# Attention ordered by whole batches, in 24 steps of one 288-column score tile, ahead of the expert layers

## The chip, the cores and the metric

The kernel runs on one core of a Trainium2 chip. The core has five engines that run side by side, each through its own list of instructions in order: TensorE (PE, matrix products; PEld is its weight load), VectorE (DVE), ScalarE (ACT), GpSimd (POOL) and SyncE (SP), which here issues nearly all DMAs. The metric is device time in microseconds (us), the median of three runs. A profiled execution adds a trace, whose span runs from the first to the last of the program's own instructions. TensorE's clock has two levels, 1.2 and 2.4 GHz; the profile gives it as PEclk, a share of the upper one.

## The reference

Two batches of 8 heads, 576 positions, 64 numbers per head, all float32. Heads 0 to 3 are local (a query sees itself and the 31 keys before it), heads 4 to 7 strided (a query sees earlier keys whose position is the same modulo 32). The attention output, 1152 tokens of 512 numbers, goes through a mixture of four experts and then through a gated layer.

```python
mask_local   = (rel >= 0) & (rel < 32)
mask_strided = (rel >= 0) & (pos[None, :] % 32 == pos[:, None] % 32)
attn = softmax(where(mask, scale * q @ k.T, -1e9))
x = attn @ v                              # -> (1152, 512)
for e in range(4):                        # w1[e]: 512x1024, w2[e]: 1024x512
    out += p[:, e:e + 1] * (relu(x @ w1[e]) @ w2[e])
return (sigmoid(out @ w_gate) * (out @ w_val)) @ w_out   # float64 weights, width 1536
```

## The kernel before, in words

**Products.** Each factor of the expert and gate products is scaled by a power of two and split into a high and a low float16 part, and each product is three matmuls (high by high, high by low, low by high; `split_products`, lines 585 to 587). There are 4560 of these, called products below; all but 336 have 288 columns.

**Units.** The tokens form four chunks T of 288. The products come in 56 units, each written as a generator: ("u", s, T) is the first matrix of expert s (or, from s = 4 on, the gate and value matrices), ("d", s, T) the second. A u unit has 8 tiles of 12 products, a d unit of an expert 4 tiles of 24, so 96 products each. Units are numbered in program order: 0 to 7 are expert 0 (u and d of chunk 0, then of chunk 1, and so on); from 8 on the u unit of one chunk is followed by the d unit of an earlier one. A tile ends in its evacuation from PSUM: in a u unit ACT writes the high part and a float32 copy and POOL the low part (lines 624 to 626); in a d unit DVE scales the tile (line 645) and, from expert 1 on, POOL adds it to the sum `x2acc` (line 647).

**Weights.** Weight pieces (0 and 1 are the matrices of expert 0, 2 and 3 of expert 1, up to 7; 8 to 16 are the float64 thirds of the gated layer) are prepared by `prep_weights`, a generator of which `prep_some` advances up to two steps per call, at one point of every tile. A piece of an expert takes four maxima on DVE (line 308, two per 1 MB half `raw`), then a step that folds them (line 310), a PE transpose of the result (line 246), a PE product that spreads it (line 252), and then the conversion of four parts of 1024 columns: ACT scales, ACT casts to the high part, POOL subtracts for the low part (lines 339, 340, 342). The four steps around the transpose return "hold", which ends that call. Only three halves fit in the `raw` buffers, so the second half of a piece is loaded into the place of a half of the piece before, when that has been converted. The prepared weights live in two pools of two places; `has_room` holds a piece back until the unit number has passed `free_after`, the last use of the piece whose place it takes. For the second pool's first two pieces (2 and 3) that is N_ATT - 1, here 5.

**Attention.** It runs as a generator of steps, one `attend()` each. Step i normalizes the tile of step i-1, multiplies by the values for a step four (or three) back, transposes the weights of the step three (or two) back, transposes q and k of a later step, and computes the scores of its own. One step's softmax is a chain: a mask and the scores on PE into one PSUM tile, row maximum and subtraction on DVE (lines 413, 414), exponential on ACT, row sum, an added constant and a reciprocal on DVE (lines 457 to 459), multiplication by it on POOL (line 460). Attention is cut by chunk: chunk 0 takes 4 tiles-steps and a drain and stands alone at the start; the other chunks' steps are laid into units 0 to 3, one after every 6 (later 9) groups of three products. Local heads take 96 queries by 128 keys, one score tile per head, so two tiles to a step. In the stretch ahead of unit 0 each step is followed by 6 matmuls on zeros (`keep_warm`, line 170). `x_pair` scales a chunk's attention output and splits it (lines 517, 518).

**Loads.** q, k and v come by chunk; for local heads with 256-byte pieces. SP takes its DMAs strictly in order. The token weights `pb` (line 221) sit in four buffers, and a later one waits on SP until DVE has read the one whose place it takes.

Of the kernel before, what the change touches and what calls it, by code (L numbers as in the profile page):

```python
# [26 lines left out]
PSUM_BUFS = 3  # L27
PB_BUFS = 4
ATT_LATER = 9
WARM = 11  # L30
WARM_STEP = 6
ATT_EVERY = 6
# [3 lines left out]
def attn_moe_glu_kernel(ctx, tc, q, k, v, dp, w1, w2, wg, wv, wo, out):  # L36
# [13 lines left out]
    TL = TC // 3  # L50
# [6 lines left out]
    accp = ctx.enter_context(tc.tile_pool(name="accp", bufs=1))  # L57
# [8 lines left out]
    sp_ = at_stack.enter_context(tc.tile_pool(name="sps", bufs=2, space=PSUM, side="right", reuse_waits="tile"))  # L66
# [5 lines left out]
    def load_strided_qk(T, c):  # L72

        b, part = divmod(T, 2)
        h0 = 4 + 2 * c
        for nm, src in (("qs", q), ("ks", k)):
            t = atp.tile([NC, 2, 8 * D], F32, tag=nm, name=nm, bufs=3)
            nc.sync.dma_start(
                t, src[b, h0:h0 + 2, part * TC:(part + 1) * TC].rearrange("h (u r) d -> u h (r d)", r=8))
            qkv[nm, T, c] = t  # L80

    def load_strided_v(T, eng):
        b, part = divmod(T, 2)
        for c in range(2):
            h0 = 4 + 2 * c
            if part == 0:
                qkv["vs", b, c] = atp.tile([NU, 2, 8 * D], F32, tag="vs", name="vs", bufs=3)
            eng.dma_start(
                qkv["vs", b, c][part * NC:(part + 1) * NC],
                v[b, h0:h0 + 2, part * TC:(part + 1) * TC].rearrange("h (u r) d -> u h (r d)", r=8))  # L90

    def load_local(T, c, eng):

        b, part = divmod(T, 2)
        for nm, src in (("ql", q), ("kl", k)):
            t = qkv[nm, T, c] = atp.tile([TL, 3, 2, D], F32, tag=nm, name=nm, bufs=2)
            for x in range(2):
                eng.dma_start(
                    t[:, :, x, :], src[b, 2 * c + x, part * TC:(part + 1) * TC].rearrange("(i p) d -> p i d", p=TL))

    def load_vl(T, eng):

        b, part = divmod(T, 2)
        t = atp.tile([128, 4, 3, D], F32, tag="vl", name="vl", bufs=2)
        for h in range(4):
            i0 = 0
            if part == 0:
                eng.dma_start(t[:, h, 0, :], v[b, h, 0:128, :])
                i0 = 1
# [344 lines left out]
    def group_norm(g):  # L454
        for pp, sm, n, w, m, to_sum in soft[g]:
            if to_sum:
                nc.vector.tensor_reduce(sm, pp, AX.X, ALU.add)
# [496 lines left out]
```

## Time and profile before

| what | value |
|---|---|
| time, median of 3 runs | 778.07 us (775.97 to 778.96) |
| profiled execution, its own time | 779.5 us |
| span of the profiled execution | 777.7 us |
| PE, DVE, ACT, POOL busy | 719.1, 387.5, 296.2, 306.6 us |
| mean granted TensorE clock | 0.95 of 2.4 GHz |
| bytes moved by DMA | 48.76 MB, 63 GB/s over the span |

Matmuls overlap in the pipeline, so a PE that reads as busy can still run at half its clock; the granted clock has to be read beside it. The busy share is a mean over stages that differ, so the stages are what to read: the stretch ahead of the first product, the units that share PE with attention, and the rest.

### The profile page before, as it was taken

The numbers are of one execution on the slowest core, as the hardware profiler recorded it, in microseconds if no ns is written. First come the engines' busy times: TensorE is split into PE (matmuls) and PEld (weight loads), VectorE is DVE, ScalarE is ACT, GpSimd is POOL, SyncE is SP. The second block draws the span as 40 slices with busy tenths as digits, with TensorE's granted clock in tenths as the row PEclk, the third lists the DMA queues.
The fourth block names the chain that finished last, engine by engine and source line by source line (L and its number), as shares of the span: only waits on it lengthen the run. The fifth ranks groups of instructions, "written<-read, shape, count | busy, mean of one in ns | idle before, by whom it ended". The sixth has DMA issues, their size and how long they took to land.

```text
span 777.7 us, 13784 instructions
## 1 busy us (share of the span) xinstructions
PE 719.1 (92%) x5727; PEld 528.1 (68%) x5727; DVE 387.5 (50%) x778; ACT 296.2 (38%) x618; POOL 306.6 (39%) x326
## 2 busy tenths in 40 slices
PE   8886788999988899979999998987989999999998
PEld 5545566677766677757777776765766666676774
DVE  2755365453224141125821967575967967922122
ACT  1343643353374841634315232522333344141220
POOL 2213631231374873735835554534142433231110
PEclk7988696999999999989999999899999999999999
DMA  8705451000033330030410213030303211000001
GB/s 175 182 10 162 114 133 35 1 2 8 9 109 116 109 117 8 1 116 15 167 52 9 84 41 109 2 108 1 109 1 109 64 46 55 1 1 1 28 28 69
DMA packets 34590, 48.76 MB, mean 63 GB/s; under 512 B 18684, under 2 KB 21024, under 8 KB 34528
## 3 DMA queue, kind: packets, MB, share of 16 engines
q1 hardware_dynamic: 33312, 47.59, 20.2%
q8 instruction: 45, 0.74, 0.4%
q10 hardware_dynamic: 1216, 0.30, 0.2%
q14 instruction: 17, 0.14, 0.1%
HBM read 45.50 MB, written 2.38 MB: 62 GB/s over the span
## 4 chain that ended last, share of the span: by engine, by line
PE 65%; DVE 14%; POOL 7%; ACT 6%; DMA 4%; issue 3%; SPq 0%; POOLq 0%; DVEq 0%; ACTq 0%
PE gps L585 19%; PE gps L586 19%; PE gps L587 18%; POOL wl L342 4%; DMA raw<-in_moe_w_dram 3%; DVE pk L308 3%; POOL hl L626 2%; POOL x2acc L647 2%; PE sps L402 1%; PE o L501 1%; DVE cv L279 1%; PE warm L170 1%; DVE bits L275 1%; ACT wh L340 1%; DVE bits L277 1%
## 5 line engine op out<-in xcount | busy, mean ns | idle before, releaser
L585 PE MATMUL gps<-xh,wh 128*128 128x288 f16 x896 | 263.1, 294 | 2.1 <-ACT xh L517 2.1
L586 PE MATMUL gps<-xl,wh 128*128 128x288 f16 x896 | 263.0, 294 | 0.3 <-DVE xl L518 0.3
L587 PE MATMUL gps<-xh,wl 128*128 128x288 f16 x896 | 262.7, 293 | 0.0
L586 PEld LDWEIGHTS <-wh 128*128 128x128 f16 x1408 | 140.4, 100 | 40.1 <-issue 2.4
L587 PEld LDWEIGHTS <-wl 128*128 128x128 f16 x1408 | 140.4, 100 | 39.2 <-issue 1.1
L585 PEld LDWEIGHTS <-wh 128*128 128x128 f16 x1408 | 140.1, 99 | 39.4 <-issue 0.3
L626 POOL TENSOR_TENSOR hl<-t,hh 128x288 f16<-128x288 f32 x128 | 100.7, 795 | 130.8 <-ACT t L625 121.7
L586 PE MATMUL gps<-hl,wh 128*128 128x288 f16 x512 | 148.0, 289 | 0.3 <-POOL hl L626 0.2
L585 PE MATMUL gps<-hh,wh 128*128 128x288 f16 x512 | 148.1, 289 | 0.0
L587 PE MATMUL gps<-hh,wl 128*128 128x288 f16 x512 | 148.0, 289 | 0.0
L624 ACT ACTIVATE hh<-gps 128x288 f16<-128x288 f32 x128 | 52.3, 409 | 165.3 <-PE gps L587 165.2
L723 POOL TENSOR_TENSOR hl<-t,hh 128x288 f16<-128x288 f32 x48 | 37.5, 781 | 139.7 <-ACT hh L722 139.7
L342 POOL TENSOR_TENSOR wl<-raw,wh 128x1024 f16<-128x1024 f32 x30 | 65.2, 2175 | 17.5 <-ACT wh L340 14.7
L645 DVE SCALAR_TENSOR_TENSOR t<-gps,comb,pb 128x288 f32<-128x288 f32 x48 | 24.6, 513 | 93.5 <-PE gps L587 86.9
L647 POOL TENSOR_TENSOR x2acc<-x2acc,t 128x288 f32<-128x288 f32 x48 | 40.3, 840 | 63.7 <-DVE t L645 60.1
L625 ACT ACTIVATE t<-gps 128x288 f32<-128x288 f32 x128 | 51.9, 405 | 14.5 <-POOL hl L626 14.5
L308 DVE TENSOR_REDUCE pk<-raw 128x1 f32<-128x1024 f32 x32 | 37.6, 1210 | 34.2 <-DMA raw<-in_moe_w_dram 34.2
L460 POOL TENSOR_TENSOR P<-P,sm 96x384 f32<-96x384 f32 (+1 forms) x28 | 21.0, 755 | 84.8 <-DVE sm L459 62.6
L722 ACT CAST hh<-t 128x288 f16<-128x288 f32 x48 | 20.7, 431 | 80.8 <-DVE t L721 80.8
L721 DVE SCALAR_TENSOR_TENSOR t<-gps,sg 128x288 f32<-128x288 f32 x48 | 21.8, 455 | 54.7 <-PE gps L587 42.1
L342 POOL TENSOR_TENSOR wl<-cv,wh 128x1024 f16<-128x1024 f32 x18 | 40.1, 2226 | 19.1 <-ACT wh L340 19.1
L714 ACT ACTIVATE sg<-gps,comb 128x288 f32<-128x288 f32 x48 | 23.9, 499 | 47.8 <-PE gps L587 39.1
(125 smaller groups left out, 869.1 us busy)
## 6 DMA issues: line engine op xcount, KB each, us to landing
raw<-in_moe_w_dram SPq DMA_DIRECT2D x16, 1024.0 KB
raw<-in_moe_w_gate_dram SPq DMA_DIRECT2D x6, 1024.0 KB
raw<-in_moe_w_val_dram SPq DMA_DIRECT2D x6, 1024.0 KB
raw<-in_moe_w_out_dram SPq DMA_DIRECT2D x6, 1024.0 KB
pb<-pd SPq DMA_DIRECT2D x15, 144.0 KB
out_dram<-outacc SPq DMA_DIRECT2D x8, 256.0 KB
qs<-in_q_dram SPq DMA_DIRECT2D x8, 144.0 KB
ks<-in_k_dram SPq DMA_DIRECT2D x8, 144.0 KB
```

Of the source, the lines that this page charges most:

```text
L308: nc.vector.tensor_reduce(pk[:, n:n + 1], part, AX.XY, ALU.max, apply_absolute_value=True)
L342: nc.gpsimd.tensor_tensor(lo_, part, hi_, ALU.subtract)
L585: nc.tensor.matmul(ps, ah, bh, start=i == 0, stop=False)
L586: nc.tensor.matmul(ps, ah, bl, start=False, stop=False)
L587: nc.tensor.matmul(ps, al, bh, start=False, stop=i == n - 1)
L624: nc.scalar.activation(hh[fb], ps, AF.Relu, scale=DOWN)
L625: nc.scalar.activation(t, ps, AF.Relu, scale=DOWN)
L626: nc.gpsimd.tensor_tensor(hl[fb], t, hh[fb], ALU.subtract)
L645: nc.vector.scalar_tensor_tensor(t, ps, cc, pb[e, T], ALU.mult, ALU.mult)
L647: nc.gpsimd.tensor_tensor(a, a, t, ALU.add)
L714: nc.scalar.activation(sg, pg, AF.Sigmoid, scale=comb[:, col:col + 1])
L723: nc.gpsimd.tensor_tensor(dl, gv, dh, ALU.subtract)
```

## The change

Attention is cut by batch instead of by chunk. Each batch has 12 steps (strided heads in three steps per pair, local heads in three steps per pair), each with one score tile of 288 columns: 24 steps, with no drain between batches. A local tile now holds 64 queries by 96 keys of both heads of a pair. Local q and k are loaded in pieces of 1536 bytes, six positions to a partition; their transposition is six plain products with the identity per half, and the copies out of PSUM put the positions in order. All of batch 0 (steps 0 to 17, with the first steps of batch 1) stands ahead of unit 0, with 5 matmuls on zeros after each step; ten more steps go into unit 0, one after every 3 groups of three products; what is left runs before unit 1. `x_pair` now serves two chunks with one scale.

Besides: the low part of an expert's weights is made on DVE in one instruction from the raw half, so ACT does one instruction per part and POOL none; the sum `x2acc` is added on DVE; N_ATT is 1, so pieces 2 and 3 have room from unit 1 on; PSUM has 2 instead of 3 banks for products and 3 instead of 2 for scores while attention lasts.

```diff
-PSUM_BUFS = 3
+PSUM_BUFS = 2
-ATT_LATER = 9
-WARM_STEP = 6
-ATT_EVERY = 6
+WARM_STEP = 5
+ATT_EVERY = 3
+BLOCK = 64
+LEAD = 32
...
+    def load_local_qk(b, c):
+        for nm, src in (("ql", q), ("kl", k)):
+            t = qkv[nm, b, c] = atp.tile([TL, 2, 6 * D], F32, tag=nm, name=nm, bufs=2)
+            nc.sync.dma_start(t, src[b, 2 * c:2 * c + 2].rearrange("h (p i) d -> p h (i d)", i=6))
...
             hi_, lo_ = wh[i][at], wl[i][at]
-            if early and n % 2 == 0:
+            if dt == F32:
                 nc.scalar.activation(hi_, part, AF.Copy, scale=up[:, i:i + 1])
                 nc.vector.scalar_tensor_tensor(lo_, part, up[:, i:i + 1], hi_, ALU.mult, ALU.subtract)
                 yield
...
+                    pv_ = ps[:, :3 * TL].rearrange("p (i n) -> p i n", i=3)
+                    for x in range(3):
+                        i = 3 * half + x
+                        for y in range(2):
+                            nc.tensor.matmul(
+                                pv_[64 * y:64 * y + 64, x, :], src[:, y, i * D:(i + 1) * D], ident[:TL, :TL],
+                                start=True, stop=True)
+                    frm = ps[:, :3 * TL].rearrange("p (i n) -> p n i", i=3)
+                    dst = to[:, :S].rearrange("p (n i) -> p n i", i=6)[:, :, 3 * half:3 * half + 3]
+                if nm == "q":
+                    nc.scalar.activation(dst, frm, AF.Copy, scale=SCALE)
+                else:
+                    nc.vector.tensor_copy(dst, frm)
+                yield
...
+        for b in range(B):
+            for c in range(2):
+                tasks.append((len(gs), qk_tasks("s", b, c)))
+                gs += [("s", b, c, 0, (0, 1)), ("s", b, c, 1, (0,)), ("s", b, c, 1, (1,))]
+            for c in range(2):
+                tasks.append((len(gs), qk_tasks("l", b, c)))
+                gs += [("l", b, c, t, (0, 1)) for t in range(3)]
+        n = len(gs)
+        ends = {n // B * (b + 1) - 1 + 4: b for b in range(B)}
...
+            if 0 <= i - 1 < n:
+                norm(gs[i - 1])
+            if 0 <= i - 4 < n:
+                values(gs[i - 4])
+            if 0 <= i - 3 < n:
+                transposes(gs[i - 3])
+            do_tasks(i)
+            if i < n:
+                scores(gs[i])
...
             if e:
-                nc.gpsimd.tensor_tensor(a, a, t, ALU.add)
+                nc.vector.tensor_tensor(a, a, t, ALU.add)
...
-    N_ATT = len(units) - 2
+    N_ATT = 1
...
         while 0 not in x_done:
             i = attend()
             keep_warm(WARM_STEP)
-            for _ in range(2):
-                if i >= 3 and (going or todo[0] == 0):
-                    prep_some(0, 1)
-        keep_warm(WARM_STEP)
+            if i >= 8 and (going or todo[0] == 0):
+                prep_some(0, 1)
         for n, u in enumerate(units):
-            while u[2] not in x_done:
-                attend()
+            if n == 1:
+                while "p" not in tmp:
+                    if attend() is None:
+                        end_attention()
...
-                    if n_none % (ATT_LATER if 1 in x_done else ATT_EVERY) == 0 and attend() is None:
+                    if n_none % ATT_EVERY == 0 and attend() is None:
                         end_attention()
```

How the change moves instructions is seen at three places. The first is PE's list inside unit 0, at the first step that is laid between products. Before, it is a step of chunk 1 (a strided tile, and transposes of local q and k):

```order
L472 MATMUL tps<-ident,P 72x128 x4
L384 MATMUL qkps<-ident,ql 128x96 x3
L384 MATMUL qkps<-ident,kl 128x96 x3
L398 LDWEIGHTS identb
```

Now it is step 18, of batch 1:

```order
L459 MATMUL o<-PT,vs 64x36 x16
L433 MATMUL tps<-ident,P 36x128 x8
L371 MATMUL qkps<-ident,ql 64x96 x6
L371 MATMUL qkps<-ident,kl 64x96 x6
L393 LDWEIGHTS identb
L393 MATMUL sps<-ml,identb 128x288
L407 MATMUL sps<-klT,qlT 64x96 x6
```

Such a step stands after every 9 products of unit 0 instead of after every 18 of units 0 to 3, and it holds one score tile whether its heads are local or strided.

The second place is SP's list of DMAs around the last weights of the experts (`raw` from `in_moe_w_dram`; 128x4x512 are halves of a second matrix, 128x2x1024 of a first one). Before:

```order
L138 DMA raw<-in_moe_w_dram 128x4x512
L221 DMA pb<-pd 128x288 x3
L138 DMA raw<-in_moe_w_dram 128x4x512
L138 DMA raw<-in_moe_w_gate_dram 128x2x512
L221 DMA pb<-pd 128x288
```

And now:

```order
L126 DMA raw<-in_moe_w_dram 128x4x512
L212 DMA pb<-pd 128x288 x2
L126 DMA raw<-in_moe_w_dram 128x4x512
L126 DMA raw<-in_moe_w_gate_dram 128x2x512
L212 DMA pb<-pd 128x288 x2
```

The second half of piece 7 (the second `raw` row of each) stood behind three loads of `pb` and now stands behind two; the third, which waits for the end of unit 14, comes after it.

The third place is DVE's list in unit 26, the d unit of the last expert and chunk 0, with its last tile and the maximum over the chunk. Before:

```order
L645 SCALAR_TENSOR_TENSOR t<-gps,comb,pb 128x288
L649 TENSOR_REDUCE peak<-x2acc 128x1
L657 TENSOR_REDUCE peak<-peak 128x1
```

And now:

```order
L611 SCALAR_TENSOR_TENSOR t<-gps,comb,pb 128x288
L613 TENSOR_TENSOR x2acc<-x2acc,t 128x288
L615 TENSOR_REDUCE peak<-x2acc 128x1
L623 TENSOR_REDUCE peak<-peak 128x1
```

The addition, which stood on POOL between the first two rows, is now DVE's own.

## Rows read from the trace of the kernel before

**Rows 1.** Windows by stage: length, busy (count) by PE, PEld, DVE, ACT, POOL; clock.

```profile
0.00:53.70 53.70, 45.97 (x399) 27.75 (x400) 25.69 (x65) 18.06 (x42) 9.06 (x27) 0.87 0.58 133
53.70:184.10 130.40, 111.47 (x1097) 82.73 (x1097) 66.48 (x178) 54.41 (x143) 40.69 (x49) 0.84 0.26 67
184.10:443.40 259.30, 244.59 (x1943) 191.65 (x1941) 96.11 (x152) 116.60 (x230) 145.93 (x141) 0.97 0.20 67
443.40:583.80 140.40, 127.10 (x987) 98.20 (x985) 98.81 (x201) 47.77 (x96) 60.63 (x60) 0.96 0.16 54
583.80:777.70 193.90, 189.94 (x1310) 127.80 (x1307) 100.43 (x186) 59.41 (x109) 50.30 (x51) 1.00 0.11 40
269.80:281.60 11.80, 11.80 (x99) 9.43 (x97) 3.75 (x5) 7.23 (x9) 11.35 (x8) 1.00 0.27 91
```

**Rows 2.** Timeline of PE: start, length, line, operation; steps ahead of unit 0.

```profile
11.67 2.74 PE L170 MATMUL warm<-const-float32-0.0 128*128 128x512 bf16 x6
...
24.52 1.13 PE L501 MATMUL o<-PT,vs 36*64 36x36 f32 x32
25.57 1.05 PE L472 MATMUL tps<-ident,P 128*36 128x128 f32 x8
26.46 0.49 PE L427 MATMUL sps<-ml,identb 96*96 96x384 bf16 x2
26.88 0.90 PE L431 MATMUL sps<-klT,qlT 64*96 64x128 f32 x12
27.71 1.48 PE L170 MATMUL warm<-const-float32-0.0 128*128 128x512 bf16 x6
...
38.72 0.68 PE L368 MATMUL qkps<-ident,qs 36*128 36x36 f32 x8
...
44.58 0.72 PE L402 MATMUL sps<-ksT,qsT 64*64 64x72 f32 x16
```

**Rows 3.** Groups by line and shape on DVE: busy us, mean ns, idle before.

```profile
L308 DVE TENSOR_REDUCE pk<-raw 128x1 f32<-128x1024 f32 x32 | 37.6, 1210 | 34.2 <-DMA raw<-in_moe_w_dram 34.2
...
L518 DVE SCALAR_TENSOR_TENSOR xl<-xf,up,xh 128x288 f16<-128x288 f32 x16 | 7.6, 532 | 6.2 <-ACT xh L517 6.2
L414 DVE TENSOR_TENSOR P<-sps,nm 128x288 f32<-128x288 f32 x12 | 5.5, 458 | 1.5 <-DVE nm L413 0.5
...
L413 DVE TENSOR_REDUCE nm<-sps 128x4 f32<-128x288 f32 x8 | 3.6, 450 | 3.8 <-PE sps L402 3.7
L457 DVE TENSOR_REDUCE sm<-P 128x4 f32<-128x288 f32 x8 | 3.5, 440 | 0.5 <-ACT P L415 0.5
...
L336 DVE SCALAR_TENSOR_TENSOR wl<-raw,up,wh 128x1024 f16<-128x1024 f32 x2 | 2.6, 1285 | 2.8 <-ACT wh L335 2.8
...
L459 DVE RECIPROCAL sm<-sm 128x4 f32<-128x4 f32 x8 | 1.4, 178 | 0.3
```

**Rows 4.** Timeline: a PE transpose in unit 8; SP's loads of token weights.

```profile
245.96 0.37 PE L246 MATMUL gps<-ident,pk 128*1 128x128 f32 x1 [3.54 <-DVE pk L310]
...
282.37 47.88 SPq L221 DMA_DIRECT2D pb<-pd  x3
```

**Rows 5.** Timeline: DVE, POOL, PE after unit 26's last product (479.3).

```profile
480.92 0.51 DVE L645 SCALAR_TENSOR_TENSOR t<-gps,comb,pb 128x288 f32<-128x288 f32 x1
...
481.50 0.79 POOL L647 TENSOR_TENSOR x2acc<-x2acc,t 128x288 f32<-128x288 f32 x1 [2.32 <-DVE t L645]
...
482.33 0.45 DVE L649 TENSOR_REDUCE peak<-x2acc 128x1 f32<-128x288 f32 x1 [0.90 <-POOL x2acc L647]
...
483.12 0.27 PE L246 MATMUL gps<-ident,peak 128*1 128x128 f32 x1 [2.31 <-DVE peak L657]
```

**Rows 6.** Timeline: one DVE line, with POOL at work and without.

```profile
469.66 2.12 POOL L626 TENSOR_TENSOR hl<-t,hh 128x288 f16<-128x288 f32 x2
...
471.22 1.11 DVE L277 SCALAR_TENSOR_TENSOR bits<-raw,bits 128x512 uint32<-128x512 uint32 x1
...
479.59 0.68 DVE L277 SCALAR_TENSOR_TENSOR bits<-raw,bits 128x512 uint32<-128x512 uint32 x1
```

More of the change, by code (lines that the diff above doesn't have):

```diff
@@ L92, in load_local @@
[L92 to L109, printed above, removed]
-            k0 = part * TC + 96 * i0 - 32
-            src = v[b, h, k0:k0 + 128, :]
-            eng.dma_start(t[:, h, i0:3, :], bass.AP(src.tensor, src.offset, [[D, 128], [96 * D, 3 - i0], [1, D]]))
-        qkv["vl", T] = t
+            t = qkv[nm, b, c] = atp.tile([NU, 2, 8 * D], F32, tag=nm, name=nm, bufs=2)
@@ L395, in scores_strided, with scores @@
+    def scores(g):
+        kind, b, c, part, hs = g
+        if kind == "s":
+            w = NC * (part + 1)
+            m = 4 * len(hs)
+            mask = (mask_s2 if part else mask_s)[:, :w].unsqueeze(1).to_broadcast([128, m, w])
+        else:
+            w, m = WIN, 3
+            mask = mask_l[:, 0 if part == 0 else 1:, :][:, :3, :]
         ps = sp_.tile([128, 512], F32, tag="s", name="sps")
         pv_ = ps[:, :m * w].rearrange("p (a b) -> p a b", b=w)
-        mask = (mask_s2 if part else mask_s)[:, :w]
@@ L409, in scores_strided @@
-        nm = atp.tile([128, 8], F32, tag="nm", name="nm", bufs=4)
-        sm = atp.tile([128, 8], F32, tag="sm", name="sm", bufs=6)
-        pt = atp.tile([128, 384], F32, tag="P", name="P", bufs=6)
+        nc.tensor.matmul(pv_, identb, mask, start=True, stop=False)
+        qt, kt = QT[kind, b, c], KT[kind, b, c]
+        for j in range(m):
+            for x in range(2):
+                lo = 64 * x
+                rows = slice(lo, lo + 64)
+                if kind == "s":
+                    at = (4 * hs[0] + j) * NU
+                    lhsT = qt[rows, at + part * NC:at + part * NC + 64]
+                    rhs = kt[rows, at:at + w]
+                else:
+                    at = (3 * part + j) * BLOCK
+                    lhsT = qt[rows, at:at + BLOCK]
+                    rhs = kt[rows, at:at + w]
+                nc.tensor.matmul(pv_[rows, j, :], lhsT, rhs, start=False, stop=j == m - 1)
@@ L553, in attention, with do_tasks @@
+        n = len(gs)
+        ends = {n // B * (b + 1) - 1 + 4: b for b in range(B)}
+        running = []
+        def do_tasks(i):
+            left = 2
+            while tasks and (tasks[0][0] <= i + 1 or (tasks[0][0] <= i + 3 and left > 0)):
+                if next(tasks[0][1], "end") == "end":
+                    tasks.pop(0)
+                else:
+                    left -= 1
+        do_tasks(-1)
+        for i in range(n + 8):
             for x in list(running):
@@ L913, in attn_moe_glu_kernel @@
                 go_late(NT - 1)
-                acc["out"] = accp.tile([128, NTB, DM], F32, tag="acc", name="outacc")
+                acc["out"] = tmp["acc"].tile([128, NTB, DM], F32, tag="acc", name="outacc")
             load_p_some(n)
```

367 lines of the change are left out of this document (145 added, 222 removed).

## The prediction

> **What bounds the kernel now.** I read the stages first [rows 1], because the busy shares of the whole span mix a PE that is full with one that waits. The last row there, one d unit with nothing around it, is the measure: 96 products, PE busy 11.80 of 11.80 us, clock 1.00. A unit costs 11.8 us when nobody waits. The stage from 583.8 on has clock 1.00 and PE busy 189.94 of 193.90 us; the change does not reach it, so it stays 193.9. The 34 units before it would take 34 x 11.8 = 401.2 us, but end at 583.8. The other 182.6 us lie in four places: 53.7 ahead of the first product; 130.4 - 47.2 = 83.2 in units 0 to 3, which share PE with attention; 259.3 - 236.0 = 23.3 in units 4 to 23; 140.4 - 118.0 = 22.4 in units 24 to 33.
>
> In the first two stages the clock is 0.87 and 0.84 and PE is busy 45.97 of 53.70 and 111.47 of 130.40 us. PE works most of the time there, but a good part of it at the lower clock, and stops to wait for the softmax of a step. The nine steps ahead of unit 0 cost 6.0 us each, the 21 in units 0 to 3 on average 83.2 / 21 = 4.0 us.
>
> In units 4 to 23, PE, which takes its list in order, stands at the transpose of a weight piece's maxima until DVE has them [rows 4]: 3.54 us in unit 8. There are four such waits (units 6, 8, 9, 15). With the lower clock that follows some of them they make up most of the 23.3 us, so 5.8 each. In unit 15 the cause is on SP: three loads of `pb`, which must wait for a reader, occupy the queue from 282.37 for 47.88 us, and the weights behind them come late.
>
> In units 24 to 33 PE waits for the maximum of an expert sum [rows 5]: 2.31 us in unit 27, one of four (units 27, 29, 30, 32). The chain hands the tile from DVE to POOL and back, and DVE sits idle 0.90 us at every tile meanwhile, so that it begins the last tile 1.6 us after PE has finished (480.92 against 479.3).
>
> **The start, ahead of unit 0.** Now 18 steps stand there instead of nine. PE's prices at the upper clock [rows 2]: 32 value products 1.05 us (from one row's start to the next), 8 transposes of weights 0.9, a mask 0.2, 12 local scores 0.83, 16 strided scores 0.7 (32 short ones I take as 1.1), 5 matmuls on zeros 1.2 (6 take 1.48), 4 transposes of q or k 0.35. A half of local q or k is now six plain products, which no row shows; between 0.35 and the 0.90 of local scores, I take 0.6, since they have fewer columns than those scores.
>
> Before, the first zeros begin at 11.67. Two more copies of q and k now precede them: 13.7. At the lower clock the zeros of step 0 cost 2.3 (6 took 2.74), step 1 costs 3.2 and 2.3 more for zeros, then step 2 at the upper clock 2.1: 23.6. Steps 3 to 7, added from the list, are 4.6, 4.8, 2.6, 5.4 and 4.9, together 22.3, and DVE has less than that: 45.9.
>
> From step 8 on the first weight piece is prepared beside attention and DVE has more than PE. Each of the ten steps 8 to 17 has a maximum 0.45, subtraction 0.46, sum 0.44 and two short ones of about 0.2, so 1.75 [rows 3], 17.5 in all; four weight maxima at 1.21 are 4.8; three low parts at 1.29, 3.9; four splits of x at 0.53, 2.1; eight copies out of PSUM, priced like the subtraction, 3.7; three maxima over 576 columns at 0.9, 2.7; small ones 2. That is 36.7 us against 33 for PE from the list. Each engine also waits for the other. In the first stage before, time over PE busy was 53.70 / 45.97 = 1.17 [rows 1]; with that factor 43 us. The first product comes at 89, 35 us later than before.
>
> **Unit 0.** Ten steps, 18 to 27, one per 9 products. PE: 11.8 for products and 16 for attention, 28. DVE has 33 before unit 1 may begin: six full steps 10.5, one sum 0.9, four splits 2.1, six weight maxima 7.3, five low parts 6.4, four copies 1.9, three wide maxima 2.7, small ones 1.2. With 1.17: 38 us. Unit 1 begins at 127. The last two splits of x run under its products. Before, four units had been done by 184.1; now units 1 to 3 add 35.4, so the same point comes at 162 without further waits.
>
> **Weights.** An expert's piece loses one ACT instruction and the POOL subtraction per part; DVE gets one of 1.29 us instead. It needs two calls for conversion, not four. POOL's hand-over leaves the chain, and pieces 2 and 3 need not wait for unit 6. What decides is the distance on PE between the call that converts the half whose place is reused and the transpose behind it. By the order of the program it is 96 products or more for pieces 2, 4, 5, 7 and 8 (11.8 us) and 60 (7.4 us) for piece 3, in unit 2, and piece 6, in unit 9. In between must fit the conversion of two parts (2.6 on DVE after ACT), the load and two maxima (2.4). The load's time is the unknown; I expect 7.4 to be too short and 11.8 enough, so two waits of 5.8 remain: one in units 1 to 3, one in units 4 to 23. The bounds are no wait at all and one for each of five pieces, 0 to 29 us. In SP's list piece 7's second half no longer stands behind the `pb` load that waited for unit 14, so unit 15's wait goes.
>
> The DVE instruction reads two tiles in SBUF while POOL works on the low parts of a unit. The trace shows what that can cost [rows 6]: the same DVE instruction takes 0.68 us alone and 1.11 beside POOL, 0.43 more. On four parts that is 1.7 us per piece, which counts only in the two waits: 3 us in all, within the range.
> The Trainium skill, page "SBUF — State Buffer", section "Who interferes with whom", says that DVE with two SBUF inputs and GpSimd share a port, and that whichever starts second is blocked until the first is done. The two rows agree; by that rule the sum below would be about 3 us higher.
>
> **The addition on DVE.** It costs 48 times about 0.46 (like the subtraction of the same size), with no wait behind it in experts 1 and 2. In expert 3, scaling 0.51, addition 0.46 and maximum 0.45 follow each other without the idle 0.90. DVE is then on time at the last tile, and the chain ends 1.7 us after the last product instead of 3.8. In units 27 and 29 twelve products, 1.5 us, cover it, so these waits and their lower clock go; in units 30 and 32 nothing stands between, and about 2 us remain. With waits for gate weights left as they are, I take 12 instead of 22.4 us (bounds 5 and 22.4).
>
> **Sum.** 127 + 35.4 + 5.8 (units 1 to 3), 236 + 5.8 + 0.8 (4 to 23), 118 + 12 (24 to 33), 193.9 behind: 734.7 us of span. The profiled execution's own time was 1.8 above its span and the median of the runs 1.4 below that execution, so 735.
>
> **Rivals.**
> 1. *PE alone sets the pace.* If DVE's work hides, the factor falls away: 23.6 + 22.3 + 33 + 28 = 107 for the start and unit 0, 20 us less, 715. For it: in steps at the upper clock without weights PE runs from group to group without a gap [rows 2]. Against it: DVE's list is the longer one from step 8 on.
> 2. *Steps cost what they cost.* A step is a chain over four engines; with before's 6.0 us per step ahead of unit 0 and 4.0 inside, the first product comes at 108 and unit 1 at 108 + 11.8 + 40 = 160: 768. For it: both averages are measured. Against it: they hold two score tiles per local step, drains and late loads.
> 3. *The waits stay.* The loads remain late and DVE, which took over POOL's work, is late itself: 23.3 and 22.4 as before instead of 6.6 and 12, nothing saved there: 27 us more, 762.
> 4. *Slower: the clock stays low while attention lasts.* PE's short float32 pieces with waits between them ran at 0.84 to 0.87 before [rows 1]. At 1.2 GHz throughout, steps 3 to 17 take 2 x 55 and unit 0 2 x 28: unit 1 begins at 190 and the time is 798. It decides from a begin of unit 1 at 127 + 43 = 170 on. Against it: 5 matmuls on zeros in every step, and no long idle on PE by the sums above.
>
> **How the numbers follow.** Forecast 0.52 (its own range 722 to 750), rival 1 0.12, rival 2 0.16, rival 3 0.13, rival 4 0.06, no change to speak of 0.01. The range 715 to 767 holds the forecast and rival 3, about half of rival 1 and most of rival 2, so eight in ten; the ends leave out the corners where several bounds fall together. Less than 0.5% either way, 4 us, cannot be told from no change. Faster 0.91, same 0.03, slower 0.06.
>
> **What would show it.** First product near 89 and first product of unit 1 near 127: the start and unit 0 are right. A clock above 0.9 in the first 89 us: rival 4 is out. In units 1 to 23, PE waits at the piece transposes in units 2 and 9 alone. At the transposes of the expert maxima in units 27 and 29 waits under 0.5 us, in 30 and 32 about 2. The stage after unit 33 at 193.9. The prediction is wrong if unit 1 begins after 150, or if DVE, with POOL's work on top, makes PE wait where it did not before.

## The result, and the profile after

The changed kernel takes 735.62 us (median of 4 runs, 735.24 to 741.38) where the kernel before took 777.58 in the same comparison (775.97 to 778.96): a ratio of 0.948, 95% interval 0.943 to 0.953. The forecast was 735. The profiled execution took 735.24 us, its span is 733.5. One of the six runs of the experiment called unit 0's front, at 746.44 us, was in a slower state and is left out of its median below.

The stages, from the windows of both traces [rows 1] and the forecast's sum:

| stage | before | forecast | after |
|---|---|---|---|
| ahead of the first product | 53.7 | 89 | 79.9 |
| unit 0 | | 38 | 44.9 |
| units 1 to 3 | | 41.2 | 40.8 |
| all up to unit 4 | 184.1 | 168.2 | 165.6 |
| units 4 to 23 | 259.3 | 242.6 | 241.5 |
| units 24 to 33 | 140.4 | 130 | 131.6 |
| behind unit 33 | 193.9 | 193.9 | 194.8 |

The windows of the changed kernel, the stages first and then three pieces of the first one (the low clock, steps 3 to 7, steps 8 to 17), with the columns of [rows 1] (start:end, length, busy time of PE, PEld, DVE, ACT, POOL, granted clock, DMA share, GB/s):

```profile
0.00:79.90 79.90, 73.40 (x949) 49.66 (x962) 49.44 (x130) 27.20 (x62) 16.47 (x46) 0.98 0.53 139
79.90:124.80 44.90, 34.77 (x431) 25.43 (x431) 37.33 (x78) 22.29 (x53) 10.46 (x16) 0.94 0.31 108
124.80:165.60 40.80, 37.37 (x296) 28.95 (x296) 29.92 (x50) 17.66 (x33) 8.73 (x9) 0.99 0.30 104
165.60:407.10 241.50, 238.10 (x1937) 189.18 (x1936) 104.17 (x176) 82.41 (x194) 73.50 (x89) 1.00 0.17 55
407.10:538.70 131.60, 122.50 (x986) 96.02 (x984) 109.14 (x220) 47.35 (x96) 44.24 (x39) 1.00 0.17 58
538.70:733.50 194.80, 190.00 (x1310) 127.84 (x1308) 101.10 (x187) 59.84 (x110) 50.62 (x51) 1.00 0.11 40
...
9.80:13.20 3.40, 3.07 (x21) 1.99 (x18) 1.74 (x5) 0.76 (x2) 0.53 (x1) 0.50 0.94 241
17.10:39.30 22.20, 21.47 (x335) 15.62 (x338) 13.09 (x34) 6.81 (x16) 3.78 (x9) 1.00 0.94 232
39.30:79.90 40.60, 36.80 (x493) 25.11 (x498) 29.97 (x79) 16.38 (x38) 6.45 (x14) 1.00 0.16 47
```

The clock column and the PE column are to be read together. From unit 1 on the clock is 0.99 to 1.00; before it was 0.84 to 0.97 up to unit 33. POOL's 145.93 us in units 4 to 23 have become 73.50, and PE waits less although DVE has more to do. The first stage is a PE stage: busy 73.40 of 79.90 us. Unit 0 is the only stage in which DVE is busier than PE.

What PE waited for in units 1 to 23 (us in total, times, longest), from the view of waits:

```profile
PE gps L237 <- DVE pk L301: 5.1, 3, 2.8
PE gps L552 <- POOL hl L592: 1.7, 1, 1.7
```

The transposes at line 237 are those of the weight pieces; their three waits lie in units 2 (1.7), 9 (2.8) and 15 (0.6). Unit 8, which waited 3.54 us [rows 4], has none.

Three places from the timelines of ACT, DVE and PE:

```profile
83.70 2.17 ACT L325 ACTIVATE wh<-raw,up 128x1024 f16<-128x1024 f32 x2
85.78 1.80 ACT L489 ACTIVATE xh<-xf,up 128x288 f16<-128x288 f32 x4
87.49 0.67 ACT L438 COPY PT<-tps 36x288 f32<-36x288 f32 x2
87.91 0.91 PE L371 MATMUL qkps<-ident,ql 96*64 96x96 f32 x12 [3.40 <-ACT PT L438]
...
119.28 2.34 DVE L299 TENSOR_REDUCE pk<-raw 128x1 f32<-128x1024 f32 x2
121.53 0.74 DVE L475 TENSOR_REDUCE peak<-xf 128x1 f32<-128x576 f32 x1
122.31 0.16 DVE L480 TENSOR_REDUCE peak<-peak 128x1 f32<-128x4 f32 x1
122.52 0.37 PE L237 MATMUL peaks<-ident,peak 128*1 128x128 f32 x1 [3.44 <-DVE peak L480]
...
442.75 0.69 DVE L270 SCALAR_TENSOR_TENSOR cv<-magn,bits 128x512 f32<-128x512 uint32 x1
443.36 0.51 DVE L611 SCALAR_TENSOR_TENSOR t<-gps,comb,pb 128x288 f32<-128x288 f32 x1
443.90 0.46 DVE L613 TENSOR_TENSOR x2acc<-x2acc,t 128x288 f32<-128x288 f32 x1
444.40 0.45 DVE L615 TENSOR_REDUCE peak<-x2acc 128x1 f32<-128x288 f32 x1
444.88 0.16 DVE L623 TENSOR_REDUCE peak<-peak 128x1 f32<-128x4 f32 x1
445.19 0.27 PE L237 MATMUL gps<-ident,peak 128*1 128x128 f32 x1 [0.69 <-DVE peak L623]
```

At 83.70 two conversions of weights and four splits of x stand in ACT's list ahead of the copies that empty PSUM, and PE waits 3.40 us. At 119.28 two maxima of the next weight piece stand ahead of the maximum that PE waits for, 3.44 us. Both are in unit 0. The last six rows answer to [rows 5]: scaling, addition and maximum follow on one engine, without the idle 0.90 us of the hand-over, and the wait in unit 27 is 0.69 instead of 2.31.

### The profile page after: what moved, and what is told of

It is laid out like the page before. It is cut to its first block, busy times and chain, and to the rows that moved or that the text cites. A ratio compares the mean times of both kernels' runs of the same rounds, so it can differ in the third digit from the quotient of the medians.

```text
span 733.5 us, 13980 instructions
## 1 busy us (share of the span) xinstructions
PE 696.1 (95%) x5899; PEld 517.1 (70%) x5911; DVE 431.1 (59%) x836; ACT 256.7 (35%) x544; POOL 204.0 (28%) x249
## 3 DMA queue, kind: packets, MB, share of 16 engines
HBM read 45.63 MB, written 2.38 MB: 65 GB/s over the span
## 4 chain that ended last, share of the span: by engine, by line
PE 77%; DVE 15%; ACT 5%; issue 2%; POOL 1%; ACTq 0%; DVEq 0%; POOLq 0%
PE gps L551 22%; PE gps L552 22%; PE gps L553 21%; DVE pk L299 3%; PE warm L158 3%; PE sps L407 2%; DVE wl L326 2%; ACT wh L325 2%; PE qkps L371 1%; PE tps L433 1%; DVE cv L270 1%; PE o L459 1%; DVE x2acc L613 1%; DVE t L611 1%; DVE bits L268 1%
## 5 line engine op out<-in xcount | busy, mean ns | idle before, releaser
L552 PE MATMUL gps<-xl,wh 128*128 128x288 f16 x896 | 256.7, 286 | 1.1 <-DVE xl L490 1.1
L551 PE MATMUL gps<-xh,wh 128*128 128x288 f16 x896 | 256.9, 287 | 0.3 <-ACT xh L489 0.3
L553 PE MATMUL gps<-xh,wl 128*128 128x288 f16 x896 | 256.6, 286 | 0.0
L592 POOL TENSOR_TENSOR hl<-t,hh 128x288 f16<-128x288 f32 x128 | 105.0, 825 | 247.8 <-ACT t L591 247.6
L553 PEld LDWEIGHTS <-wl 128*128 128x128 f16 x1408 | 138.0, 98 | 38.2 <-issue 3.2
L551 PEld LDWEIGHTS <-wh 128*128 128x128 f16 x1408 | 137.8, 98 | 36.1 <-issue 0.2
L552 PEld LDWEIGHTS <-wh 128*128 128x128 f16 x1408 | 137.9, 98 | 35.6 <-issue 0.8
L689 POOL TENSOR_TENSOR hl<-t,hh 128x288 f16<-128x288 f32 x48 | 37.5, 782 | 145.4 <-ACT hh L688 145.4
L611 DVE SCALAR_TENSOR_TENSOR t<-gps,comb,pb 128x288 f32<-128x288 f32 x48 | 24.6, 513 | 83.6 <-PE gps L553 82.1
L326 DVE SCALAR_TENSOR_TENSOR wl<-raw,up,wh 128x1024 f16<-128x1024 f32 x32 | 40.8, 1314 | 35.7 <-ACT wh L325 35.7
L551 PE MATMUL gps<-wh,hh 128*128 128x512 f16 (+1 forms) x112 | 41.6, 371 | 0.0
L552 PE MATMUL gps<-wl,hh 128*128 128x512 f16 (+1 forms) x112 | 41.6, 371 | 0.0
L553 PE MATMUL gps<-wh,hl 128*128 128x512 f16 (+1 forms) x112 | 41.6, 371 | 0.0
```

Source lines behind the costliest of these rows:

```text
L326: nc.vector.scalar_tensor_tensor(lo_, part, up[:, i:i + 1], hi_, ALU.mult, ALU.subtract)
L551: nc.tensor.matmul(ps, ah, bh, start=i == 0, stop=False)
L552: nc.tensor.matmul(ps, ah, bl, start=False, stop=False)
L553: nc.tensor.matmul(ps, al, bh, start=False, stop=i == n - 1)
L592: nc.gpsimd.tensor_tensor(hl[fb], t, hh[fb], ALU.subtract)
L611: nc.vector.scalar_tensor_tensor(t, ps, cc, pb[e, T], ALU.mult, ALU.mult)
```

## The experiments

Each time stands beside runs of the kernel before; the ratio to it has its 95% interval. The stages of each run come from its own trace. The changed kernel's own ratio is 0.948 (0.943 to 0.953).

**One part undone: the addition on POOL.**

```diff
-                nc.vector.tensor_tensor(a, a, t, ALU.add)
+                nc.gpsimd.tensor_tensor(a, a, t, ALU.add)
```

> The changed kernel, except that the sum x2acc is added on POOL again. Theory (the hand-over from DVE to POOL and back made PE wait at the maxima of the expert sums): the waits at the transposes of these maxima grow again by 1.5 to 2 us each in units 27, 29, 30 and 32, with some time at the lower clock behind them; units 24 to 33 go from 131.6 back to 138 to 141 us, the rest stays (units 4 to 23 at 241.5), time 742 to 745. Rival (units 24 to 33 got shorter because POOL no longer has the low parts of the weights, and DVE or POOL is on time anyway): units 24 to 33 stay at 131 to 133, time 735 to 737.

Measured 746.61 us, ratio 0.960 (0.955 to 0.966). Window of units 24 to 33:

```profile
408.30:547.80 139.50, 127.23 (x987) 98.19 (x985) 98.79 (x201) 47.78 (x96) 60.36 (x60) 0.96 0.16 55
```

139.5 instead of 131.6, units 4 to 23 at 240.7. The waits at the maxima are 10.3 us in all instead of 6.2, and the granted clock is 0.96 instead of 1.00. The theory holds for these units (138 to 141 expected), though the median lies above its 742 to 745. Of the 7.9 us, 3.2 are more idle time of PE and 4.7 more busy time, with three stretches at the lower clock. The wait of 0.61 us in unit 15 is absent in this run: it is what the addition costs when it stands on DVE.

**One part undone: low parts of weights by ACT, ACT, POOL.**

```diff
-            if dt == F32:
+            if early and n % 2 == 0:
                 nc.scalar.activation(hi_, part, AF.Copy, scale=up[:, i:i + 1])
```

> The changed kernel, except that the low part of an expert's weights is made as before by two ACT instructions and a subtraction on POOL, so that a part takes two advances of the generator again. Theory (the number of advances decides how far apart conversion, load and transpose stand on PE): pieces 2 and 3 move from units 2 and 3 to units 3 and 4, pieces 5 and 6 each get one more tile of distance, and the transpose in unit 9 stands 96 products behind the one in unit 8 as after the change; single waits of 1 to 3 us appear or grow, units 4 to 23 go from 241.5 to 244 to 252 us. Unit 0 gets longer by 2 to 6 us, because ACT, which already makes PE wait there, has one more instruction of about 1 us per part. Units 24 to 33 stay at 131.6. Time 739 to 750. Rival (what helped in units 4 to 23 was the earlier room for pieces 2 and 3 and nothing else): units 4 to 23 stay at 241 to 243, unit 0 alone grows, time 736 to 741. Other rival (DVE is the crowded engine and gains from giving the work away): unit 0 gets shorter by 2 to 5 us, time 730 to 734.

Measured 766.37 us, ratio 0.984 (0.978 to 0.990): more than any theory gave. Units 4 to 23 take 259.5, all that the change had gained there, units 1 to 3 46.1 and unit 0 47.1. Timelines of POOL, SP, DVE and PE, in units 8, 9 and 14:

```profile
221.11 4.27 POOL L332 TENSOR_TENSOR wl<-raw,wh 128x1024 f16<-128x1024 f32 x2 [1.38 <-ACT wh L330]
230.52 0.34 SPq L212 DMA_DIRECT2D pb<-pd  x1
231.40 0.93 SPq L126 DMA_DIRECT2D raw<-in_moe_w_dram  x2
237.30 2.35 DVE L299 TENSOR_REDUCE pk<-raw 128x1 f32<-128x1024 f32 x2 [4.56 <-DMA raw<-in_moe_w_dram]
239.89 0.37 PE L237 MATMUL gps<-ident,pk 128*1 128x128 f32 x1 [4.08 <-DVE pk L301]
...
249.17 2.14 POOL L332 TENSOR_TENSOR wl<-raw,wh 128x1024 f16<-128x1024 f32 x1
251.34 5.93 SPq L126 DMA_DIRECT2D raw<-in_moe_w_dram  x2
256.32 2.34 DVE L299 TENSOR_REDUCE pk<-raw 128x1 f32<-128x1024 f32 x2 [10.03 <-DMA raw<-in_moe_w_dram]
...
315.66 9.05 POOL L332 TENSOR_TENSOR wl<-raw,wh 128x1024 f16<-128x1024 f32 x4 [1.38 <-ACT wh L330]
316.31 1.80 DVE L613 TENSOR_TENSOR x2acc<-x2acc,t 128x288 f32<-128x288 f32 x1
```

This is the path of a piece. Two subtractions on POOL free a half, a load takes its place, DVE reads it, and PE waits for DVE. Two different steps hold it up. In unit 8 the half is free at 225.38, but its load leaves only at 231.40, because a `pb` load stands ahead of it on SP, and that one waits until DVE has read the last tile of unit 7 (to 230.49). Units 4 and 15 are alike. These three units are 4.4, 6.9 and 5.4 us longer than in the changed kernel, 16.7 of the 18.0 us that units 4 to 23 lose. In unit 9 no `pb` load is in the way: the load leaves 0.03 us after the second subtraction, so there the conversion itself is on the path, and unit 9 is 1.3 us longer. For two parts POOL takes 4.27 us where DVE now takes 2.47, and ACT's two instructions per part (1.15 and 1.04) take as long as POOL's one. How late in the program the load is issued, and so what stands ahead of it on SP, is my theory of the number of calls. It fits most of the loss, but with a size I had not expected. The edit changes calls and engines at once, so their shares are not shown apart; the old instructions in two calls would have told. Five waits at transposes make 17.5 us in units 1 to 23, and the clock is 0.82 and 0.91 in units 8 and 15. Of the 30 us, 4.8 lie ahead of unit 0, where the clock was at half from 71.6 to 81.7.

**One part undone: room for pieces 2 and 3 from unit 6.**

```diff
-    N_ATT = 1
+    N_ATT = len(units) - 2
```

> The changed kernel, except that pieces 2 and 3 have room only from unit 6 on (N_ATT as before). Theory (pieces 2 to 5 are then prepared one right behind the other in units 6 to 9, each waiting for the load of its second half): waits of 2 to 4 us at the transposes in units 6, 8 (two) and 9, those in units 2 and 3 gone; units 1 to 3 go from 40.8 to 38 to 40, units 4 to 23 from 241.5 to 248 to 256 us, time 739 to 748. Rival (distances are kept by the faster conversion alone): units 4 to 23 stay within 1 us of 241.5, time 733 to 736.

Measured 741.68 us, ratio 0.953 (0.949 to 0.957). Units 1 to 3 take 36.7, units 4 to 23 249.9, with four waits of 8.7 us in all in units 6, 8, 9 and 15, the last of them the 0.61 that the changed kernel has too. The theory holds (units 1 to 3 gain a little more than its 38 to 40, and one wait in unit 8 came, not two), and the net of these stages is 8.4 - 4.1 = 4.3 us; the other 2.1 of the span lie ahead of unit 0, in code that is the same.

**The side edits alone, in the kernel before.** The three edits above, made in the kernel that has attention by chunks.

> The kernel before with the three side edits alone (addition on DVE, low part of an expert's weights on DVE in one instruction, N_ATT 1), attention by chunks as before. Theory (gains add up by stage): units 24 to 33 take about 131.6 us, units 4 to 23 242 to 250 us, and unit 4 begins at about 184 (180 to 188) as before, since attention sets that; time 750 to 760, so that the reordering of attention is worth some 18 to 22 us of the 42. Rival (the reordering is what frees the engines for the side edits): units 4 to 23 stay at 255 to 260 and the time at 765 to 772. Other rival (the side edits also help attention, by taking the casts from ACT): unit 4 begins at 170 to 178, time 740 to 748.

Measured 755.64 us, ratio 0.971 (0.966 to 0.975). Windows ahead of unit 0, to unit 4, of units 4 to 23 and 24 to 33:

```profile
0.00:50.60 50.60, 43.24 (x393) 26.97 (x400) 26.23 (x64) 17.38 (x42) 9.07 (x27) 0.87 0.59 141
50.60:175.60 125.00, 105.86 (x1098) 79.83 (x1098) 72.74 (x184) 48.28 (x137) 29.50 (x43) 0.90 0.27 70
175.60:428.40 252.80, 242.32 (x1942) 190.81 (x1941) 125.97 (x204) 92.05 (x206) 74.79 (x89) 0.99 0.22 69
428.40:560.00 131.60, 122.51 (x986) 96.02 (x984) 109.13 (x220) 47.32 (x96) 44.26 (x39) 1.00 0.17 58
```

The time fits the theory, the stages do not. Unit 4 begins at 175.6, not 184, as the other rival said (170 to 178); most of this lies in unit 0, which takes 39.1 instead of 44.2 us, and its cause was not tested. Units 4 to 23 take 252.8, 11.3 more than in the changed kernel. By span, the side edits alone are worth 777.7 - 754.4 = 23.3 us and the new attention on top 20.9: 10.0 ahead of unit 4, 11.3 behind it. The second part is indirect. By the code the second pool of weights exists only when attention has ended, so with attention in units 0 to 3 its room comes late whatever N_ATT is, and waits of 1.3, 5.7 and 2.9 us stand in units 7, 8 and 9. The longest of them, in the timelines of DVE, SP and PE:

```profile
221.31 2.48 DVE L335 SCALAR_TENSOR_TENSOR wl<-raw,up,wh 128x1024 f16<-128x1024 f32 x2 [0.80 <-ACT wh L334]
227.07 0.34 SPq L221 DMA_DIRECT2D pb<-pd  x1
227.51 0.93 SPq L138 DMA_DIRECT2D raw<-in_moe_w_dram  x2
234.66 2.35 DVE L308 TENSOR_REDUCE pk<-raw 128x1 f32<-128x1024 f32 x2 [5.37 <-DMA raw<-in_moe_w_dram]
237.25 0.37 PE L246 MATMUL gps<-ident,pk 128*1 128x128 f32 x1 [5.67 <-DVE pk L310]
```

Here DVE converts, in 2.48 us, and the half is free at 223.79. The load still leaves only at 227.51, behind a `pb` load. So fast conversion alone does not end this wait; the order on SP has to be right as well.

**Weights of expert 0 earlier.**

```diff
-            if i >= 8 and (going or todo[0] == 0):
+            if i >= 3 and (going or todo[0] <= 1):
```

The loads move with it: the first half of piece 1 is loaded right after the first loads of v.

> The changed kernel, except that the weights of expert 0 are prepared from step 3 of attention on instead of step 8 (one advance per step), and piece 1 is begun in the same stretch; its first half is loaded right after the first loads of v. Theory (unit 0 took 44.9 us because two weight conversions and six maxima stand in ACT's and DVE's lists ahead of what the steps of attention need, while DVE has idle time before step 8): the wait of 3.4 us at the first transposes of unit 0 falls to about 1.5, DVE's work in unit 0 falls from 37.3 to 30 to 32 us, unit 0 takes 37 to 41 us; the stretch ahead of it stays at 79.9 (78 to 82), since PE with its zeros sets it; time 728 to 733. Rival (the chain of attention's own steps sets unit 0): unit 0 stays at 43 to 45, time 734 to 737. Other rival (the early work delays the chain of the first steps, in which nothing covers it): first product at 84 to 88, time 737 to 742.

Measured 736.29 us, ratio 0.947 (0.942 to 0.952): no change. Unit 0 takes 41.5, its first wait is 1.32 instead of 3.40 and DVE has 31.51 us, as the theory said, though a wait of 4.10 for a copy on ACT is new at its end. But the first product comes at 87.4, as the other rival said. Timelines of ACT and PE in the stretch ahead:

```profile
57.63 1.13 ACT L325 ACTIVATE wh<-raw,up 128x1024 f16<-128x1024 f32 x1
58.86 0.47 ACT L442 COPY PT<-tps 96x384 f32<-96x384 f32 x1
59.39 0.66 PE L363 MATMUL qkps<-ident,ks 72*128 72x72 f32 x4 [2.38 <-ACT PT L442]
```

A conversion of 1.13 us stands on ACT ahead of a copy out of PSUM for which PE waits 2.38; the exponential before it was late as well, so the conversion is only a part of that wait. From 59.6 to 66.3 the granted clock is 0.50. What was taken from unit 0 is paid ahead of it.

**No zeros, and two.** WARM_STEP = 0, and WARM_STEP = 2, instead of 5.

> The changed kernel without the 5 matmuls on zeros after each of the 18 steps ahead of unit 0 (the 11 at the very start stay). The zeros are about 20 of the 73.4 us that PE is busy there. Theory (the zeros keep the clock up, since without them PE waits for the softmax of each step): the granted clock of the stretch falls from 0.98 to 0.6 to 0.8, and what PE saves in work it loses in speed; first product at 80 to 95, time 735 to 752. Rival (PE's list with the zeros set the pace and the clock holds without them, or does not matter while DVE's 49.4 us and the chain set the pace): first product at 60 to 70, time 716 to 727.

> The changed kernel with 2 instead of 5 matmuls on zeros after each of the 18 steps ahead of unit 0, 12 us less work for PE there. Theory (zeros keep the clock up; two leave PE waiting for the softmax in part of the steps): the clock of the stretch is 0.75 to 0.9, first product at 76 to 86, time 731 to 742. Rival (the zeros are simply work on the engine that sets the pace): first product at 68 to 71, time 723 to 727.

Measured 734.70 us (ratio 0.944, 0.938 to 0.950) and 736.56 us (0.945, 0.940 to 0.950): neither can be told from the changed kernel. Without zeros:

```profile
0.00:74.70 74.70, 61.03 (x870) 46.63 (x871) 48.07 (x130) 25.11 (x62) 16.51 (x46) 0.88 0.57 148
74.70:119.80 45.10, 37.62 (x431) 27.24 (x431) 36.96 (x78) 22.59 (x53) 10.47 (x16) 0.84 0.31 104
```

The clock falls from 0.98 to 0.88, less than the theory had, and the first product comes 5.2 us earlier, at 74.7, between the theory's 80 to 95 and the rival's 60 to 70. With two zeros it comes at 80.6 at clock 0.87, as the theory of that run had it. The zeros buy clock and cost PE time of about the same amount.

**Small pieces for local q and k.**

```diff
-            nc.sync.dma_start(t, src[b, 2 * c:2 * c + 2].rearrange("h (p i) d -> p h (i d)", i=6))
+            for x in range(2):
+                nc.sync.dma_start(
+                    t[:, x, :].rearrange("p (i d) -> p i d", i=6),
+                    src[b, 2 * c + x].rearrange("(i p) d -> p i d", i=6))
...
-                    dst = to[:, :S].rearrange("p (n i) -> p n i", i=6)[:, :, 3 * half:3 * half + 3]
+                    dst = to[:, half * 3 * TL:(half + 1) * 3 * TL]
```

> The changed kernel, except that local q and k are loaded in pieces of 256 bytes again, a position to a piece (two DMAs per tensor and pair, one for each head), so that the copies out of PSUM are contiguous; work on PE, DVE and ACT has the same number of instructions. Theory (the local loads have 20 us and more until their first use, so their form is hidden, and the strided copies out of PSUM cost 0.45 to 0.47 us, the same as contiguous ones): first product at 79 to 82, time 734 to 738. Rival (small pieces hold up the queue on which the loads behind them stand, the first weights and the next batch's q and k): the first product comes 3 to 10 us later, time 739 to 746. Other rival (strided copies are the dearer part): the copies fall below 0.4 us and unit 0 gets 1 to 3 us shorter, time 731 to 734.

Measured 738.47 us (736.94 to 742.70), ratio 0.950 (0.945 to 0.955): not told apart from the changed kernel. Unit 0 is the same (45.1), the strided copy of local q on ACT costs 472 ns against 410 contiguous, eight times, that of k 459 against 456. The first product comes 4.9 us later; the window of the run with small pieces, where that arises, and the same window of the changed kernel:

```profile
71.50:81.70 10.20, 9.64 (x86) 6.77 (x88) 4.58 (x12) 2.09 (x4) 0.67 (x1) 0.50 0.01 2
```

```profile
71.50:81.70 10.20, 8.63 (x115) 5.81 (x115) 7.28 (x17) 4.77 (x10) 0.67 (x1) 1.00 0.01 2
```

The DMA share is 0.01 in both; it is the clock, which stood at half for 10.2 us, 5.1 us lost. So the loads are hidden either way in this execution; whether they had a part in the clock stays open.

**The waits of unit 0 and of the expert maxima, one by one.** Piece 2 held back until attention has ended; expert 0 prepared from step 6 on and the second split of x behind the scores; the transpose of the expert maxima one tile later; all three.

```diff
-                if i >= 2 * E and "p" not in tmp:
+                if i >= 2 and "p" not in tmp:
...
-            if i >= 8 and (going or todo[0] == 0):
+            if i >= 6 and (going or todo[0] == 0):
...
+            while second and i > ends_at[0]:
+                next(second.pop(0))
+                ends_at.pop(0)
...
         yield
+        yield
         yield from scale
```

> The changed kernel, except that piece 2 may be begun only when attention has ended, so that its first two maxima leave DVE's list at the end of unit 0. Theory (PE waits 3.44 us at the end of unit 0 for the maximum of batch 1's output, and DVE has two maxima of 2.34 us together ahead of it): the wait falls to 1.0 to 1.3 us, the time at the lower clock behind it goes, unit 0 takes 40.5 to 43 instead of 44.9 us. Pieces 2 and 3 come about one tile to one unit later; units 1 to 3 stay at 40 to 42. Time 731 to 734. Rival (DVE is late there because of the low parts of piece 1, or the maxima only move): the wait stays above 2.5 us or comes back in unit 1, time 734 to 737.

> The changed kernel with two edits at the beginning of unit 0: the weights of expert 0 are prepared from step 6 instead of step 8 of attention on (one conversion in each of the steps 14 to 17, none left at the beginning of unit 0), and the second half of the split of x stands behind the scores of its step instead of ahead of its copies out of PSUM. Theory (the wait of 3.40 us comes from ACT's list: two conversions of 2.17 and four splits of 1.80 us ahead of the copies that PE needs): the wait falls below 1 us and the low clock behind it goes; first product at 79 to 82, unit 0 39 to 42 us, time 729 to 733. Rival (as in the run with the preparation from step 3 on, a conversion on ACT holds up the copies of a step ahead of unit 0 just as well, and the low clock follows there): first product at 83 to 88, time 734 to 738.

> The changed kernel, except that the transpose of the maxima of an expert sum stands one tile, 12 products or 1.5 us, later on PE. Theory (what is left of these waits, 0.7, 1.6, 1.9 and 2.1 us in units 27, 29, 30 and 32, is DVE's chain behind the last product, which 12 products more cover): the waits fall to 0, 0.1 to 0.3, 0.3 to 0.6 and 0.5 to 0.8 us; units 24 to 33 take 126.5 to 128 instead of 131.6 us, time 730 to 733. Rival (the chain behind it, the scale and the split of the sum, is then late for the first products of units 31 to 37): the waits move there, time 735 to 738.

> The changed kernel with the edits of the three other runs of this call together (piece 2 begun only when attention has ended; expert 0 prepared from step 6 on and the second split of x behind the scores; the transpose of the maxima of an expert sum one tile later). Theory (they act at different places and add up): unit 0 takes 36 to 39 instead of 44.9 us, units 24 to 33 126.5 to 128 instead of 131.6, first product at 79 to 82; time 722 to 729. Rival (the gains at the two ends of unit 0 are given back at the waits of pieces 2 and 3, or ahead of unit 0): only the 4 us of units 24 to 33 stay, time 730 to 734.

| run | median (runs) | ratio, interval | ahead of unit 0 | unit 0 | units 24 to 33 |
|---|---|---|---|---|---|
| changed kernel | 735.62 (735.24 to 741.38) | 0.948 (0.943 to 0.953) | 79.9 | 44.9 | 131.6 |
| piece 2 later | 737.11 (733.81 to 743.91) | 0.948 (0.943 to 0.953) | 81.4 | 41.8 | 131.7 |
| unit 0's front | 739.68 (734.57 to 740.89) | 0.947 (0.943 to 0.951) | 84.9 | 41.7 | 131.6 |
| one tile later | 735.74 (733.54 to 744.13) | 0.945 (0.941 to 0.950) | 82.1 | 44.9 | 127.4 |
| all three | 735.47 (731.52 to 736.29) | 0.942 (0.939 to 0.945) | 82.2 | 42.3 | 127.4 |

Every edit does at its place what its theory said: with piece 2 later the wait of 3.44 us is 1.40, with the other front the wait of 3.40 is 0.79, with one tile more the four waits of 6.2 us are two of 1.6 together (another of 1.5 comes at the product behind). But none of the four times that the theories forecast came. Part comes back elsewhere. With piece 2 later, the wait in unit 2 is longer, 2.92 us instead of 1.74, in the timeline of PE:

```profile
148.87 0.37 PE L237 MATMUL gps<-ident,pk 128*1 128x128 f32 x1 [2.92 <-DVE pk L301]
```

There the 1.68 us for POOL in unit 3 is gone in turn, and units 1 to 3 take 40.8 as before. With the other front the clock ahead of unit 0 is at half from 75.2 to 82.0. And the column ahead of unit 0 differs where the code does not: from 8 to 17 us the granted clock is 0.81 in the changed kernel and 0.62 in the runs with piece 2 later, one tile later, the addition on POOL and late room, and their first products come at 81.4, 82.1, 81.8 and 82.0. In all three together unit 0 ran at clock 0.90 and missed its 36 to 39 us. The three together have the lowest ratio here, but its interval overlaps that of the changed kernel, so a better version is not shown.

## Why the prediction was right

The sum was 734.7 us of span and 733.5 was measured. Step by step:

**What bounds the kernel.** Right: the time lost lay in the four places named. 18.5 us came from the stages ahead of unit 4, 17.8 from units 4 to 23, 8.8 from units 24 to 33; the last stage cost 0.9.

**The start: 9 us too long.** The term had three parts. To step 2's end I took 23.6 and it was 17.1, 6.5 of the 9 us: the zeros of step 0 begin at 10.45, not 13.7, and the lower clock lasts only from 9.8 to 13.2. Some of this is luck of the execution: in four runs with the same code up to there, where the lower clock lasts longer, the first product comes 1.5 to 2.2 us later. Steps 3 to 7 were right, 22.2 against 22.3. Steps 8 to 17 took 40.6 against 43, and there the step that failed is "DVE has more than PE": DVE is busy 29.97 us where I had 36.7, PE 36.80 where I had 33. One of three low parts and all four splits of x fall behind the first product, and zeros do not hide in PE's waits. The stretch is 1.10 times PE's list, not 1.17 times DVE's; here it went the way of rival 1.

**Unit 0: 7 us too short.** The work that had slid out of the start arrived here: DVE busy 37.33 against 33. At the factor of 1.17 that is 5.1 of the 6.9 us. The factor itself is no law: it is 44.9 / 37.33 = 1.20 here, and 41.5 / 31.51 = 1.32 in the run with the weights prepared earlier. What unit 0 pays is single waits in an order of turns (3.40 behind ACT, 3.44 behind DVE) and the clock behind them. The errors of start and unit 0 are partly one, work set in the wrong stage; the rest cancelled by luck.

**Weights.** Stages right (41.2 and 242.6 against 40.8 and 241.5), the pieces of the sum mis-sized. The waits were expected in units 2 and 9 and came there, with 1.7 and 2.8 us instead of 5.8 each with the clock behind them: the clock stayed at 1.00. Not forecast were about 0.5 us for each pair of matmuls at a transpose (units 4, 8, 15 and 19 take 12.2 to 13.1), and a wait of 1.7 for POOL in unit 3. Unit 15's wait went from the list of [rows 4] as said, down to 0.6; with the low parts on POOL the three `pb` loads block SP again, for 47.36 us, and that wait is 4.8. The same cause was missed in unit 8 of the kernel before:

```profile
228.87 4.26 POOL L342 TENSOR_TENSOR wl<-raw,wh 128x1024 f16<-128x1024 f32 x2 [5.12 <-ACT wh L340]
235.65 0.34 SPq L221 DMA_DIRECT2D pb<-pd  x1
236.08 0.39 SPq L138 DMA_DIRECT2D raw<-in_moe_w_dram  x1
```

The half is free at 233.13, its load leaves at 236.08, behind `pb`. I had named SP for unit 15 alone. In the changed kernel that load leaves 0.03 us after its conversion and the `pb` load comes behind it:

```profile
205.82 3.20 SPq L126 DMA_DIRECT2D raw<-in_moe_w_dram  x2
214.42 0.34 SPq L212 DMA_DIRECT2D pb<-pd  x1
```

**The port.** Three us were forecast; the conversion on DVE takes 1.314 us in the mean of 32 against 1.285 [rows 3], 1 us in all. The effect itself is real where POOL's instruction is long: in the run with low parts on POOL the addition on DVE takes 1.80 us beside POOL's subtraction and 0.46 alone: it begins 0.65 us behind the subtraction and ends 0.32 us after it. The Trainium skill, page "SBUF — State Buffer", section "Who interferes with whom", says that whichever of the two begins first holds the shared port for its whole length and the other is blocked; these rows agree. What the term left out are the additions: the 48 of the changed kernel take 25.6 us, not 22, because five of them meet a subtraction on POOL.

**The addition.** Right in size (130 against 131.6) and shown by undoing it (139.5). Wrong in units 27 and 29, where waits of 0.7 and 1.6 stayed against the 0.5 allowed: the step "DVE is then on time at the last tile" failed, because steps of the float64 conversion stand in between (442.75 above).

**The signs.** One sign of being wrong was that DVE, with POOL's work on top, makes PE wait where it did not before. It came in small: the maximum of batch 1's output makes PE wait 3.44 us where such a maximum had cost 1.9 at most after the first product, behind two maxima of weights that DVE had to make before as well. Besides units 2 and 9, PE waited in unit 15 (0.6) and, for POOL, in unit 3 (1.7).

**Rivals.** The waits did not stay (rival 3). The clock did not stay low (rival 4), 0.98 and 0.94; even without zeros it is 0.88, so the zeros were not needed against it. Steps ahead of unit 0 cost 79.9 / 18 = 4.4 us, not 6.0 (rival 2).

## What to carry to other kernels

When a cheap step ends a chain that frees a buffer, count the whole way to the next reader, with what stands ahead of the load in its queue: the low parts, taken back to ACT and POOL, cost 30 us of span, and most of what units 4 to 23 lost stood in three units whose load left behind a `pb` load. Edits that share a chain don't add up: side edits 23.3 us, attention on top 20.9, but the three side edits taken back one by one cost 8.2, 29.9 and 6.5 us of span, 44.6 together. And where engines take turns in order, work moved out of one stall tends to make the next one; look at what stands directly ahead of the copy that PE needs.

## What the runs showed of the hardware

The same wait can cost its length or several times that. At the transpose of the attention maximum ahead of unit 0 PE waits 1.21 us in the changed kernel and in the run with small pieces. In the one the clock stays at 1.00 behind it, in the other it is 0.50 for 10.2 us. At the transpose in unit 9 both wait 2.79 us; behind it the clock is 1.00 in the one and 0.50 for 3.4 us in the other. The times of one kernel go with its mean clock: in the run with the transpose one tile later the six times are 733.5 and 733.8 us at a mean clock of 0.991, 734.8 and 736.7 at 0.986, 738.1 at 0.979 and 744.1 at 0.972. That such waits are what differs there is not shown, since only one execution of each kernel has a trace. A stage of one trace is therefore known, by my estimate from the 4.9 us of the run with small pieces, to about 5 us where it has waits, and differences of that size need the cause in the rows, not the time alone.
